# Batch 4's second FFN product by block products, and a new order of pieces, in an attention and maxout FFN kernel

## The chip, the cores and the metric

The kernel runs on one core of a Trainium2 chip. The metric is the device time of one execution in microseconds. The kernel before was timed in three runs: 163.65, 163.83 and 164.19 us, median 163.83. One further execution was profiled; it took 164.42 us.

A core has five engines with a queue of instructions each, in program order: TensorE (PE in the profile, with its weight loads as PEld) multiplies and writes to PSUM; VectorE (DVE), ScalarE (ACT) and GpSimd (POOL) do elementwise work; SyncE (SP) issues transfers. An instruction waits for semaphores before it starts, and whatever is queued behind it on its engine waits too.

## The reference

Inputs are q, k, v of shape (8 batches, 8 heads, 576 positions, 64) and phi of shape (8, 8, 576, 32), in float32. Per batch and head:

```python
a = softmax(phi, axis=2)              # over the 576 positions
k_m = a^T k ; v_m = a^T v             # (32, 64) each
attn = softmax(q k_m^T / 8, axis=-1)  # (576, 32)
o = attn v_m
```

The heads of a position are joined to a row x of 512, which gives 4608 rows, and then

```python
h = np.maximum(np.maximum(x @ w1, x @ w2), x @ w3)   # 512 -> 768
out = h @ w_out                                      # 768 -> 512
```

## The kernel before

The product of attn with v_m is never formed. Since x is attn times v_m, v_m is folded into the weights: per batch, small products of v_m with w1 - w3 and w2 - w3 give `wp`, and with w3 w_out give `wp3`. Then max(x w1, x w2, x w3) = x w3 + max(x (w1 - w3), x (w2 - w3), 0), so that FFN1 has two products instead of three (one evacuated with a Relu, the other with a max against it), and FFN2 adds attn times `wp3` to h times w_out.

The work is cut into pieces with names of a letter, a number and a batch. The same piece, such as `F8@2`, is a call of one helper. The order of all pieces is written out by hand as one list (line 758 on), and each engine's queue holds its instructions in the order of that list. A `!` behind a piece swaps the engine of its elementwise part. The letters that matter here:

- `L0` to `L3`: loads of phi, k, v, q (lines 86 to 115). They are issued by GpSimd; in two alternating buffers each, so a load waits until the batch two before has been read.
- `r0`, `r1`: packing of k and v (line 105), GpSimd, ScalarE when swapped. `E`: exponential of phi (232), ScalarE.
- `B`: the products a^T k and a^T v with their denominators (250). `N`: their normalisation on VectorE (263 to 292). `K`: transposes of the result on TensorE and an evacuation (294).
- `Q0`, `Q1`: transposes of q on VectorE (315). `S`: scores on TensorE (335) and two exponentials on ScalarE (344).
- `a`, `s`, `c`, `m`, `X`: the second softmax's transposition, sum, reciprocal (VectorE), product (`m`, line 411, GpSimd) and transposition back (VectorE, 419), in two halves 0 and 1.
- `D0` to `D3`: folds (442), evacuated mostly by ScalarE. `F0` to `F11`: FFN1 (468); an even number is evacuated with a Relu (ScalarE, VectorE when swapped), an odd one with the maximum (VectorE, 481).
- `T0` to `T4`: FFN2 of a tile of 128 positions (658, 667, 676), evacuated by either engine (EVAC at 167), and written to memory through SyncE. `T4` is the tile in the middle that two neighbouring batches share.

For the 512 positions of batches 5 and 6 outside `T4`, FFN2 is done as a two by two block product with seven products instead of eight. `U` combines the blocks of the weights (`combine_w`, 507; batch number 9 is for the shared w_out), `A0` to `A3` the blocks of h, 128 x 768, and `A4` to `A7` those of attn, 128 x 256 (`combine_a`, 552). All of them run through one helper at line 505, on GpSimd or VectorE. `P0` to `P6` (`products`, 565) are the seven products of 256 columns each (600), accumulated in place in three banks, with copies of intermediate states (612, 614) and sums into the output tile (641).

PSUM has eight banks. Which piece takes which bank is a string of digits (line 141); a piece whose bank hasn't been evacuated waits on TensorE.

Of the kernel before, what the change touches and what calls it, by code (L numbers as in the profile page):

```python
# [15 lines left out]
def kernel(  # L16
# [14 lines left out]
    B, H, S, D = q.shape  # L31
# [104 lines left out]
    for i in range(P // M):  # L136
# [4 lines left out]
    banks = iter(  # L141
        "".join(
            """
            00232204420145545045024602460260426042672643424260246024604260462342656204502406
            24062046204267240670462064260246024602064326247420640642064024620462042604605264
            620502645264034063460406064026042640246204203406767676
            """.split()
        )
    )
# [572 lines left out]
    def issue(b, n, swap):  # L722

        i = int(n[1:]) if len(n) > 1 else None
        {
            "I": lambda: [make_identity(nc, ident)]
            + [nc.gpsimd.memset(x[:, :, :, 2 * D : 2 * D + 1], 1.0) for x in kvrs],
            "Y": lambda: load_w(i) if i < 3 else load_wo(),
            "L": lambda: load_ph(b) if i == 0 else load_q(b) if i == 3 else load_kv(b, i - 1),
            "H": lambda: load_kv(b, i % 2, halves[i // 2]),  # L730
            "r": lambda: pack(b, i, swap),
            "E": lambda: [att_exp(b, h) for h in (halves if b == 0 else [slice(0, NP)])],
            "B": lambda: att_kv(b, i),
            "N": lambda: att_kv_norm(b, i),
            "K": lambda: att_kv_t(b, swap, i),
            "Q": lambda: att_q(b, i),
            "S": lambda: att_score(b),
            "a": lambda: att_t(b, i),
            "s": lambda: att_sum(b, i),
            "c": lambda: att_rec(b, i),  # L740
            "m": lambda: att_mul(b, i, swap),
            "X": lambda: (ones_mul if (b, i) in ONES else att_back)(b, i),
            "M": lambda: ones_sum(b, i),
            "R": lambda: ones_rec(b, i),
            "D": lambda: fold(b, i, swap),
            "F": lambda: ffn1(b, i, swap),
            "T": lambda: ffn2(b, i, swap),
            "U": lambda: combine_w(b, i, swap),
            "A": lambda: combine_a(b, i, not swap),
            "P": lambda: products(b, i, swap),  # L750
            "W": lambda: w3_t(i, swap),
            "O": lambda: w3_o(i, swap),
            "V": lambda: w_diff(i),
            "Z": lambda: warm_up(i),
        }[n[0]]()


    for w in """
        E@0 H2@0 H0@0 L3@0 Z25@0 B0@0 Y2@0 I@0 N0@0 Z2@0 K0@0! Q0@0 Q1@0 Z9@0 S@0 Z2@0
        M0@0 M1@0 R0@0 R1@0 W0@0 Y3@0 W1@0 W2@0 Z6@0 O1@0 H3@0 O3@0 O2@0 H1@0 X1@0 B1@0  # L760
        X0@0 N1@0 K1@0 O0@0 Y0@0 D1@0! D0@0! D3@0 F8@0 F10@0 F2@0 V0@0 F6@0 F0@0! Y1@0
        D2@0 D4@0 F4@0 L0@1 V1@0 F1@0 E@1 F3@0 L1@1 F5@0 F9@0 F7@0 L3@1 F11@0 B0@1 T3@0
        N0@1 K0@1! L2@1 Q1@1 L2@2 L1@2 Q0@1 L0@2 V2@0 T0@0! L3@2 S@1 T1@0 a0@1 s0@1 c0@1
        m0@1 B1@1 N1@1 a1@1 L1@3 K1@1 s1@1 D0@1 D1@1! D2@1 c1@1 m1@1 X0@1 L3@3 r1@2 X1@1
        T2@0! L2@3 F6@1 F10@1 F7@1 F2@1 F3@1 F4@1 F0@1 r0@2 E@2 F5@1 F1@1 F11@1 L0@3
        L0@4 F8@1 L2@4 F9@1 B@2 D3@1 N@2 Q1@2 T0@1! K@2 T2@1! r0@3 Q0@2 S@2 a0@2 a1@2
        s1@2 c1@2 m1@2 T4@1! D1@2! s0@2 D2@2 c0@2 m0@2 X1@2 D0@2 T3@1 Q0@3 L3@4 X0@2
        Q1@3 T1@1 F0@2 F4@2 F8@2 F6@2 F9@2 E@3 F7@2 F1@2 L1@4 r1@3 F10@2 F2@2 L2@5 B@3
        N@3 D3@2 F3@2 L1@5 F5@2 K@3! U0@9 F11@2 S@3 U1@9 E@4 T3@2 L0@5 T0@2! a1@3 D1@3!
        s1@3 D2@3 a0@3 r1@4 c1@3 L3@5 D0@3 T1@2 m1@3 s0@3 Q0@4 X1@3 c0@3 m0@3 X0@3 T2@2!  # L770
        F4@3! r0@4 F5@3 L2@6 F0@3 D3@3 B@4 F6@3 N@4 F1@3 F8@3 Q1@4 F2@3 F9@3 K@4! F10@3
        r1@5 F7@3 S@4 F11@3 L3@6 D3@4 E@5 r0@5 F3@3 a0@4 U3@9 L0@6 a1@4 T4@3! L1@6 L0@7
        s1@4 D0@4 D1@4! B@5 c1@4 N@5 T1@3 Q1@5 K@5 L1@7 Q0@5 s0@4 c0@4 m0@4 T3@3! S@5
        a0@5 T2@3! s0@5 a1@5 c0@5 X0@4 m1@4 X1@4 D2@4 D0@5 D1@5 m0@5 s1@5 X0@5 T0@3!
        F4@4 c1@5 F2@4 m1@5 r1@6 L2@7 F10@4 r0@6 F3@4 F5@4 F8@4 X1@5 F9@4 F0@4 F11@4
        F6@4 E@6 F10@5! F7@4 L3@7 F0@5 F2@5 A4@5! Q0@6 A5@5! F1@4 F1@5 A7@5! F8@5 F6@5
        F4@5! Q1@6 D3@5 B@6 N@6 r0@7 D2@5 T0@4! F7@5 F5@5 K@6 F3@5 U2@9 F9@5 U0@5! T1@4!
        F11@5 A0@5 A6@5 r1@7! E@7 S@6 T2@4! D1@6! U1@5! D2@6 a0@6 Q1@7 B@7 A1@5! U2@5
        U3@5 N@7 T3@4 s0@6 K@7! Q0@7 a1@6 P1@5 D3@6 s1@6 c1@6 S@7 c0@6 A2@5! m1@6 P2@5
        P4@5 a0@7 s0@7 D3@7 D2@7 m0@6 a1@7 c0@7 D1@7! P0@5! A3@5! U0@6 s1@7 P5@5 c1@7  # L780
        m1@7 X1@6 X0@6 T4@5! D0@6! D0@7 P6@5 U1@6 m0@7 F8@6 F9@6 F6@6 U3@6 U2@6 X0@7
        P3@5 F10@6 F2@6 X1@7 F11@6 F8@7 F0@6 F3@6 F7@6 F4@7 F1@6 F9@7 F4@6 A4@6 F5@6
        F2@7 F0@7 F5@7 A0@6! A6@6! A1@6! F6@7 F10@7! F3@7 A5@6! P1@6 A2@6! F1@7 P0@6
        F7@7 A3@6! F11@7 P2@6! P4@6 T0@7 T1@7 P5@6! A7@6 T4@7 P6@6! P3@6! T2@7! T3@7
    """.split():
        n, b = w.rstrip("!").split("@")
        issue(int(b), n, w.endswith("!"))
# [30 lines left out]
```

## Time and profile before

| | us |
|---|---|
| median of three runs | 163.83 |
| lowest and highest | 163.65, 164.19 |
| profiled execution | 164.42 |
| its span, first to last instruction | 162.4 |
| TensorE busy | 152.6 |
| VectorE busy | 104.5 |
| ScalarE busy | 97.8 |
| GpSimd busy | 92.2 |

The granted clock of TensorE was 0.998 on average. In the profile, L468 is a line of the kernel, PE, DVE, ACT and POOL are the engines, and a row of the timeline has the start and the length in us, then engine, line, operation, output and inputs, and in brackets the idle time before it and what ended it. In the chain of waits a row has start, length and the work that the end hung on at that time. The ends of matmuls are modelled, so their lengths overlap in the timeline; starts are exact.

### The profile page before, as it was taken

What the parts mean: (1) busy time and instruction counts of PE and PEld (TensorE: products, weight loads), DVE (VectorE), ACT (ScalarE), POOL (GpSimd) and SP (SyncE); (2) the same over time, 40 slices, a digit from 0 to 9 for tenths busy, and PEclk for the clock granted to TensorE, in tenths of its full rate; (3) what the DMA queues carried; (4) which work ended last, traced back from release to release, by engine and by line L of the source; (5) the groups of instructions that cost most, each with busy time, mean ns of one, the idle gap of its engine ahead of it and who ended that gap; (6) DMA issues with size and microseconds to landing.
All of it is one profiled execution on the core that took longest, in us unless ns stands there. A gap on an engine that the chain in (4) does not pass through costs nothing.

```text
span 162.4 us, 4946 instructions
## 1 busy us (share of the span) xinstructions
PE 152.6 (94%) x2128; PEld 90.5 (56%) x2128; DVE 104.5 (64%) x201; ACT 97.8 (60%) x144; POOL 92.2 (57%) x92
## 2 busy tenths in 40 slices
PE   7958798999798999999999999999999999999991
PEld 2433544673366535753584536776456577785570
DVE  2013703898837847577487797986999967874340
ACT  4204535934497468977689849688779786631110
POOL 7931115100598359899877964999094880395000
PEclk9999999999999999999999999999999999999999
DMA  5999999999999999999999999999221044000365
GB/s 153 152 205 208 206 211 214 276 208 210 250 323 232 212 244 378 261 237 205 261 318 230 212 312 306 286 183 174 84 96 65 4 164 160 4 0 0 129 253 199
DMA packets 21909, 31.76 MB, mean 196 GB/s; under 512 B 1152, under 2 KB 16512, under 8 KB 21888
## 3 DMA queue, kind: packets, MB, share of 16 engines
q0 software_dynamic: 16080, 21.43, 69.1%
q1 hardware_dynamic: 5664, 9.90, 17.3%
q8 instruction: 16, 0.26, 0.6%
q10 hardware_dynamic: 144, 0.13, 0.2%
q14 instruction: 5, 0.04, 0.1%
HBM read 39.32 MB, written 9.44 MB: 300 GB/s over the span
## 4 chain that ended last, share of the span: by engine, by line
PE 62%; DMA 27%; DVE 4%; POOL 3%; ACT 1%; issue 1%; POOLq 0%
PE psum L468 22%; PE psum L658 17%; DMA ph<-in_phi_dram 15%; DMA w_sb<-in_moe_w_dram 12%; PE psum L600 8%; PE psum L667 5%; PE psum L442 4%; PE psum L250 2%; POOL kvo L98 2%; PE psum L676 1%; PE psum L335 1%; DVE twb L505 1%; PE psum L699 1%; ACT e L232 1%; PE psum L300 1%
## 5 line engine op out<-in xcount | busy, mean ns | idle before, releaser
L468 PE MATMUL psum<-attn,wp 128*128 128x288 bf16 x384 | 50.2, 286 | 0.2
L468 PEld LDWEIGHTS <-wp 128*128 128x128 bf16 x384 | 36.9, 98 | 12.0 <-issue 1.5
L481 DVE TENSOR_TENSOR hT<-psum,h 128x576 bf16<-128x576 f32 x48 | 34.5, 752 | 12.7 <-PE psum L468 8.3
L658 PE MATMUL psum<-wo_sb,hT 128*128 128x512 bf16 x162 | 39.6, 380 | 0.0
L173 ACT ACTIVATE h<-psum 128x576 bf16<-128x576 f32 x43 | 26.1, 657 | 7.2 <-PE psum L468 7.1
L175 ACT CAST wp<-psum 128x1024 bf16<-128x1024 f32 (+1 forms) x30 | 28.4, 996 | 2.6 <-PE psum L442 2.6
L175 ACT COPY ot<-psum 128x512 f32<-128x512 f32 x23 | 13.6, 591 | 23.2 <-PE psum L667 18.2
L411 POOL TENSOR_TENSOR t<-t,sm 128x576 bf16<-128x576 bf16 x14 | 16.1, 1154 | 19.2 <-DVE sm L406 19.2
L108 POOL COPY kvr<-kvo 128x2304 bf16<-128x2304 bf16 x11 | 23.2, 2111 | 5.5 <-DMA kvo<-in_k_dram 4.4
L658 PEld LDWEIGHTS <-hT 128*128 128x128 bf16 x162 | 14.6, 98 | 17.8 <-issue 3.2
L667 PE MATMUL psum<-wp,attn 128*128 128x512 bf16 x46 | 13.7, 379 | 0.0
L344 ACT ACTIVATE e<-psum 128x576 bf16<-128x576 f32 x16 | 9.6, 653 | 6.1 <-PE psum L335 6.1
L162 PE MATMUL psum<-warm 128*128 128x512 bf16 x44 | 12.1, 428 | 1.2 <-DVE warm L131 1.2
L315 DVE STREAM_TRANSPOSE qT<-qq 128x576 f32<-128x576 f32 x16 | 12.0, 760 | 1.1 <-DMA qq<-in_q_dram 1.0
L232 ACT ACTIVATE e<-ph 128x1152 bf16<-128x1152 f32 (+1 forms) x9 | 9.5, 1061 | 2.9 <-DMA ph<-in_phi_dram 2.7
L98 POOL DMA_DIRECT2D kvo<-in_v_dram x9 | 6.8, 753 | 7.4 <-PE psum L250 4.1
L397 DVE TENSOR_REDUCE sm<-t 128x18 f32<-128x576 bf16 x14 | 10.4, 740 | 0.2
L113 POOL DMA_DIRECT2D qq<-in_q_dram x8 | 6.1, 759 | 6.3 <-DMA w_sb<-in_moe_w_dram 6.0
L250 PEld LDWEIGHTS <-e 64*32 64x32 bf16 x720 | 7.1, 90 | 4.5 <-issue 2.8
L389 DVE STREAM_TRANSPOSE t<-e 128x288 f32<-128x288 f32 x14 | 6.5, 468 | 4.0 <-ACT e L344 4.0
L98 POOL DMA_DIRECT2D kvo<-in_k_dram x9 | 6.9, 769 | 2.9 <-DMA qq<-in_q_dram 2.1
L419 DVE STREAM_TRANSPOSE attn<-t 128x288 f32<-128x288 f32 x14 | 6.2, 456 | 3.5 <-POOL t L411 3.5
(94 smaller groups left out, 181.0 us busy)
## 6 DMA issues: line engine op xcount, KB each, us to landing
out_dram<-ot SPq DMA_DIRECT2D x27, 256.0 KB, 6.0
qq<-in_q_dram POOLq DMA_DIRECT2D x8, 576.0 KB, 14.0
ph<-in_phi_dram POOLq DMA_DIRECT2D x7, 576.0 KB, 16.0
kvo<-in_k_dram POOLq DMA_DIRECT2D x7, 576.0 KB, 15.9
kvo<-in_v_dram POOLq DMA_DIRECT2D x7, 576.0 KB, 16.7
w_sb<-in_moe_w_dram POOLq DMA_DIRECT2D x3, 768.0 KB, 19.4
out_dram<-oj SPq DMA_DIRECT2D x4, 512.0 KB, 2.8
wo_sb<-in_moe_w_out_dram POOLq DMA_DIRECT2D x1, 768.0 KB, 15.0
```

What stands on the lines that cost most here:

```text
L98: nc.gpsimd.dma_start(out=kv[:, i, h].rearrange("p j c d -> p j (c d)"), in_=by_pair((k, v)[i], b)[:, h],)
L108: nc.gpsimd.tensor_copy(out=out_, in_=in_)
L162: nc.tensor.matmul(po[:, 0:BANK], lhsT=warm[:, 0:P], rhs=warm, start=True, stop=True)
L173: nc.scalar.activation(out=out_, in_=in_, func=AF.Relu)
L175: nc.scalar.copy(out=out_, in_=in_)
L315: nc.vector.transpose(out=s["qT"][:, j].rearrange("p j c r e -> p (j c r e)").bitcast(FP32), in_=loaded[b]["q"][:, j].rearrange("p j c d - ...
L411: (nc.vector if swap else nc.gpsimd).tensor_tensor(out=t, in0=t, in1=s["sm", g].unsqueeze(2).to_broadcast([P, S // HP, R, 2]), op=ALU.mult,)
L468: nc.tensor.matmul(acc[:, h, 0:SH], lhsT=wps[b][:, g, w * DF + ft * P : w * DF + (ft + 1) * P], rhs=attn[:, g, c0 : c0 + SH], start=(g == ...
L481: nc.vector.tensor_tensor(out=hT[:, ft, (b % 2) * S : (b % 2 + 1) * S].rearrange("p (h n) -> p h n", h=2), in0=a, in1=s["h1", ft], op=ALU.max,
L600: nc.tensor.matmul(po[:, q * CH : (q + 1) * CH], lhsT=lhs(k, q), rhs=rhs(k), start=(i < 3 and k == 0 and q == 0), stop=(k == KT and q == 1 ...
L658: nc.tensor.matmul(po, lhsT=hT[:, fc, c0 : c0 + P], rhs=wo_sb[:, fc, :], start=(n == 0), stop=False,)
L667: nc.tensor.matmul(po, lhsT=attn[:, g, c0 : c0 + P], rhs=wp3s[b][:, g, :], start=False, stop=(g == NG - 1),)
```

## The change

Only two texts of the kernel change: the list of pieces behind the first 91, and the string of banks that goes with it. FFN2 of batch 4 is no longer done by `T0@4` to `T3@4`, but by `U0@4` to `U3@4`, `A0@4` to `A7@4` and `P0@4` to `P6@4`, as batches 5 and 6 are. All other pieces stay, in another order and in part with another engine. The list grows from 402 to 417 pieces. Of the combinations, VectorE keeps one (`A6@6`) of the six it had, and the others are on GpSimd. `r0@5` goes to ScalarE beside `r1@7`. The loads behind `L1@3` come in the order v, phi, q of 3; v, k, phi, q of 4; k, phi, v of 5; k of 6, q of 5; v, phi, q of 6; phi, v, k, q of 7. Before, it was q, v, phi of 3; phi, v, q, k of 4; v, k, phi, q of 5; v, q, phi, k of 6; phi, k, v, q of 7.

```diff
-            00232204420145545045024602460260426042672643424260246024604260462342656204502406
...
+            00232204420145545045024602460260426042672643424260240642046204620160247402672062
...
-        m0@1 B1@1 N1@1 a1@1 L1@3 K1@1 s1@1 D0@1 D1@1! D2@1 c1@1 m1@1 X0@1 L3@3 r1@2 X1@1
-        T2@0! L2@3 F6@1 F10@1 F7@1 F2@1 F3@1 F4@1 F0@1 r0@2 E@2 F5@1 F1@1 F11@1 L0@3
-        L0@4 F8@1 L2@4 F9@1 B@2 D3@1 N@2 Q1@2 T0@1! K@2 T2@1! r0@3 Q0@2 S@2 a0@2 a1@2
-        s1@2 c1@2 m1@2 T4@1! D1@2! s0@2 D2@2 c0@2 m0@2 X1@2 D0@2 T3@1 Q0@3 L3@4 X0@2
...
+        m0@1 B1@1 N1@1 a1@1 L1@3 K1@1 s1@1 D0@1 D1@1! D2@1 c1@1 m1@1 L2@3 X0@1 X1@1 T2@0
+        L0@3 F0@1! F6@1 F10@1! F7@1 F8@1 F4@1 F2@1 F5@1 r1@2 r0@2 F11@1 E@2 L3@3 F9@1
+        F1@1 F3@1 B@2 U0@9 U1@9 N@2 D3@1 Q1@2 Q0@2 T1@1! K@2! r0@3 T0@1! D0@2! S@2 T4@1!
+        L2@4 a0@2 s0@2 L1@4 c0@2 a1@2 s1@2 c1@2 D2@2 D3@2 m0@2 L0@4 X0@2 m1@2 X1@2 D1@2!
+        r1@3 E@3 T3@1! T2@1! F8@2 U3@9 F10@2 F9@2 F0@2 F6@2 Q1@3 B@3 Q0@3 N@3 F2@2 F4@2
+        L3@4 L1@5 F3@2 F1@2 K@3! L0@5 F7@2 F11@2 L2@5 S@3 F5@2 a1@3 D3@3 a0@3 r1@4 s1@3
+        c1@3 r0@4 s0@3 m1@3 D0@3 E@4 T1@2 T0@2! D1@3! D2@3 c0@3 X1@3 B@4 N@4 m0@3 T2@2!
+        X0@3 Q0@4 K@4! L1@6 Q1@4 F10@3! F0@3 F2@3 F1@3 S@4 L3@5 L2@6 L0@6 U2@9 F3@3 a1@4
+        F8@3 s1@4 D3@4 U0@4 D1@4! D0@4 c1@4 a0@4 s0@4 T3@2 m1@4 c0@4 F11@3 m0@4 F9@3
+        F4@3 F6@3 X0@4 X1@4 F5@3 F7@3 F4@4! F0@4! T2@3 r0@5! E@5 F1@4 r1@5 D2@4 B@5 F2@4
...
+        A2@4! X1@5 T4@3! S@6 E@7 L3@7 A1@4! D0@6! P0@4! A3@4! a1@6 a0@6 s1@6 F6@5 A6@4!
+        F4@5 F2@5 s0@6 P1@4! F8@5 F0@5 r0@7 r1@7! P2@4 F9@5 F5@5 P4@4 c0@6 U2@5 F3@5
+        F10@5 B@7 c1@6 m0@6 U0@5 D3@6 N@7 F1@5 P3@4! K@7! F7@5 U2@4 A4@5! F11@5 P5@4
...
+        P4@6 F11@7 F5@7 P0@6 T1@7! A6@6 P3@6 T4@7 U3@6 P5@6 T2@7 P6@6 T0@7 T3@7
```

More of the change, by code (lines that the diff above doesn't have):

```diff
@@ L143 @@
             """
-            00232204420145545045024602460260426042672643424260246024604260462342656204502406
-            24062046204267240670462064260246024602064326247420640642064024620462042604605264
-            620502645264034063460406064026042640246204203406767676
+            00232204420145545045024602460260426042672643424260240642046204620160247402672062
+            40246204602406236042340620462046204602640240624026402340626024674274026402740240
+            40240420240620460247024020202406240260247204247237237
             """.split()
@@ L763 @@
         N0@1 K0@1! L2@1 Q1@1 L2@2 L1@2 Q0@1 L0@2 V2@0 T0@0! L3@2 S@1 T1@0 a0@1 s0@1 c0@1
-        m0@1 B1@1 N1@1 a1@1 L1@3 K1@1 s1@1 D0@1 D1@1! D2@1 c1@1 m1@1 X0@1 L3@3 r1@2 X1@1
-        T2@0! L2@3 F6@1 F10@1 F7@1 F2@1 F3@1 F4@1 F0@1 r0@2 E@2 F5@1 F1@1 F11@1 L0@3
-        L0@4 F8@1 L2@4 F9@1 B@2 D3@1 N@2 Q1@2 T0@1! K@2 T2@1! r0@3 Q0@2 S@2 a0@2 a1@2
-        s1@2 c1@2 m1@2 T4@1! D1@2! s0@2 D2@2 c0@2 m0@2 X1@2 D0@2 T3@1 Q0@3 L3@4 X0@2
-        Q1@3 T1@1 F0@2 F4@2 F8@2 F6@2 F9@2 E@3 F7@2 F1@2 L1@4 r1@3 F10@2 F2@2 L2@5 B@3
@@ L769 @@
[L769 to L784, printed above, removed]
+        m0@1 B1@1 N1@1 a1@1 L1@3 K1@1 s1@1 D0@1 D1@1! D2@1 c1@1 m1@1 L2@3 X0@1 X1@1 T2@0
+        L0@3 F0@1! F6@1 F10@1! F7@1 F8@1 F4@1 F2@1 F5@1 r1@2 r0@2 F11@1 E@2 L3@3 F9@1
@@ new lines @@
+        F8@3 s1@4 D3@4 U0@4 D1@4! D0@4 c1@4 a0@4 s0@4 T3@2 m1@4 c0@4 F11@3 m0@4 F9@3
+        F4@3 F6@3 X0@4 X1@4 F5@3 F7@3 F4@4! F0@4! T2@3 r0@5! E@5 F1@4 r1@5 D2@4 B@5 F2@4
+        N@5 F10@4 F8@4 Q1@5 F5@4 A4@4! F11@4 L3@6 F3@4 A5@4! F6@4 K@5! Q0@5 U1@4 A7@4!
+        T1@3! S@5 a0@5 E@6 F9@4 L0@7 s0@5 T0@3! c0@5 r0@6 F7@4 U3@4 r1@6 L2@7 m0@5 B@6
+        D2@5 D1@5! N@6 T3@3 a1@5 s1@5 L1@7 A0@4! K@6 c1@5 Q1@6 Q0@6 X0@5 D3@5 m1@5 D0@5
+        A2@4! X1@5 T4@3! S@6 E@7 L3@7 A1@4! D0@6! P0@4! A3@4! a1@6 a0@6 s1@6 F6@5 A6@4!
@@ new lines @@
+        F4@5 F2@5 s0@6 P1@4! F8@5 F0@5 r0@7 r1@7! P2@4 F9@5 F5@5 P4@4 c0@6 U2@5 F3@5
+        F10@5 B@7 c1@6 m0@6 U0@5 D3@6 N@7 F1@5 P3@4! K@7! F7@5 U2@4 A4@5! F11@5 P5@4
+        D1@7 A5@5! Q1@7 D2@7 U1@5 Q0@7 D3@7 T4@5! D1@6! m1@6 D2@6! X0@6 D0@7 A7@5! P6@4
+        X1@6 A6@5! P1@5 S@7 F4@6! P2@5! A0@5! F0@6 a1@7 a0@7 F1@6 s0@7 A1@5! c0@7 s1@7
+        P0@5 F8@6 c1@7 P4@5 A2@5! U3@5 A3@5! F10@6 m0@7 F6@6 P5@5! m1@7 F2@6 F9@6 A4@6!
+        X1@7 P3@5! U0@6 X0@7 F3@6 P6@5 F5@6 F2@7 U2@6 F7@6 F8@7 A5@6! A7@6! U1@6 F11@6
@@ L785 @@
+        F6@7 F0@7! P1@6! A0@6! F9@7 F7@7 A1@6! A2@6! A3@6! F10@7! P2@6 F3@7 F4@7 F1@7
+        P4@6 F11@7 F5@7 P0@6 T1@7! A6@6 P3@6 T4@7 U3@6 P5@6 T2@7 P6@6 T0@7 T3@7
     """.split():
```

## The prediction

> **What bounds the kernel now.** I read the page's first part, then the busy time by stretches, then the chain that ended last.
>
> ```profile
> span 162.4 us, 4946 instructions
> PE 152.6 (94%) x2128; PEld 90.5 (56%) x2128; DVE 104.5 (64%) x201; ACT 97.8 (60%) x144; POOL 92.2 (57%) x92
> ```
>
> ```profile
> 70.00:90.00 20.00, 19.93 (x297) 10.89 (x302) 14.72 (x29) 15.90 (x24) 16.91 (x13) 1.00 1.18 247
> 90.00:110.00 20.00, 20.00 (x344) 12.55 (x326) 17.18 (x34) 14.69 (x22) 16.14 (x17) 1.00 1.14 260
> 110.00:130.00 20.00, 19.95 (x310) 11.50 (x308) 18.11 (x39) 15.43 (x21) 12.99 (x11) 1.00 0.31 82
> ```
>
> Columns: stretch, length, then busy time of TensorE, weight loads, VectorE, ScalarE and GpSimd, granted clock, DMA share. TensorE has practically no idle time and the full clock, so a microsecond taken from its work, or added as a wait of it, is a microsecond of the time. The DMA engines are full (share above 1) until 110, and VectorE is the next engine to fill up: 18.1 of 20 us in the last stretch. The chain of waits gives the pieces of the TensorE stream:
>
> ```profile
> 51.36 1.17 ACT e L232
> 52.58 0.80 PE psum L250 x69
> ...
> 70.75 0.49 ACT kvt L175
> ...
> 96.92 0.77 PE psum L442 x24
> 97.70 1.40 PE psum L658 x6
> ...
> 121.03 0.53 DVE kvn L285 x2
> ...
> 133.71 8.82 PE psum L468 x72
> 142.53 0.87 PE psum L600 x8
> ...
> 147.49 1.29 PE psum L658 x6
> 148.79 0.43 PE psum L667 x2
> 149.22 1.29 PE psum L658 x6
> ```
>
> The reader sees prices (start, length). One block product (L600, eight matmuls of 256 columns): 0.87 us. One token tile of FFN2 (L658 and L667, eight of 512 columns): 149.22 - 147.49 = 1.73. Eighteen FFN1 pieces: 8.82, so 0.49 each. Behind folds, which use small tiles of the array, the first six matmuls of a token tile take 1.40, not 1.29. The links of other engines are TensorE's waits: at 51.36 the exponential of batch 2's phi, before B@2; at 70.75 ScalarE's copy of kvt, before S@3; at 121.03 VectorE's kvn, before K@7.
>
> **The change, part by part.** *TensorE's work.* T0@4 to T3@4 go: 4 x 1.73 = 6.92. P0@4 to P6@4 come: 7 x 0.87 = 6.09. Net -0.83 us, all of it on the path. A rule speaks against this. The Trainium skill (TensorE: Matmul & The Clock Gate, Back-to-back issue gap) gives a sustained spacing of about 81 ns for 128 columns and 131 ns for 512, thus an estimate near 98 ns for 256; by it 56 narrow matmuls (5.5 us) cost 1.3 us more than 32 wide ones (4.2), and the time would come out near 165.4. The trace does not agree: 0.87/8 = 109 ns and 1.73/8 = 216 ns, in proportion to the columns, for these very pieces; that case gets no chance.
>
> *Order on TensorE.* The old list comes back from small tiles to full size 25 times behind D2@1, the new one 24 times: -0.11 (1.40 less 1.29). The waits at 70.75 and 121.03 have causes that the new list removes: between K@3 and S@3 stood one FFN1 piece and now stand two; and kvn was late for K@7 because VectorE had been held for 1.5 us just before (below). By the start of the next piece they cost 0.2 each. I take -0.4 and keep 0 as the other end. The wait of B@2 stays: in front of it stand T2@0 and the same twelve FFN1 pieces, and its phi is issued in the unchanged part.
>
> *Work of the other engines.*
>
> ```profile
> L505 POOL TENSOR_TENSOR w_sb<-w_sb,hT 128x768 bf16<-128x768 bf16 x2 | 3.3, 1640 | 4.5 <-DVE w_sb L505 4.5
> L505 POOL TENSOR_TENSOR twb<-wp 128x256 bf16<-128x256 bf16 x3 | 2.1, 685 | 0.0
> L641 DVE TENSOR_TENSOR oj<-psum,snap 128x512 f32<-128x512 f32 x4 | 2.8, 692 | 0.3 <-PE psum L600 0.2
> L179 DVE CAST wp<-psum 128x1024 bf16<-128x1024 f32 x3 | 3.6, 1211 | 2.2 <-PE psum L442 2.2
> ```
>
> GpSimd: five more large combinations (1.64) and twelve more small ones (0.68), one packing copy (2.1) fewer: +14 us to 106, spread over 60 to 146. Counted along its queue, A0@4 is done 2 us ahead of P0@4, U2@4 (behind r0@7, U2@5, m0@6, U0@5) 1 us ahead of P5@4, U3@6 4 us ahead of P6@6. I cost this at nothing; if r0@7's load comes a microsecond late, that cover is gone and P5@4 waits. VectorE: three block sums, two snapshots and nine evacuations that ScalarE did (14 x 0.7), two casts (1.21); less two small copies, one block copy and five of its six own combinations (4.5 together): +7.7. ScalarE loses about 5.
>
> ```profile
> 117.81 1.64 POOL L505 TENSOR_TENSOR w_sb<-w_sb,hT 128x768 bf16<-128x768 bf16 x1 [4.52 <-DVE w_sb L505]
> 117.84 1.75 DVE L505 TENSOR_TENSOR twb<-wp,twb 128x256 bf16<-128x256 bf16 x1
> ```
>
> VectorE's small combination (a third of the large one's columns) started 0.03 us behind GpSimd's large one and ended 0.14 us behind it: it was held. The Trainium skill (SBUF — State Buffer, Who interferes with whom) has it that of two such operations the later is blocked for the whole of the first; the trace agrees. The new list leaves one on VectorE, A6@6, beside U3@6 (0.68): at most as long again, while its reader P5@6 comes some 3 us later. What is gained is VectorE's time, no TensorE time of its own: 0.
>
> *New waits.* Batch 2's normalising products stand on GpSimd behind more DMA issues:
>
> ```profile
> 57.64 2.11 POOL L108 COPY kvr<-kvo 128x2304 bf16<-128x2304 bf16 x1 [3.31 <-DMA kvo<-in_k_dram]
> 61.09 2.27 POOL L411 TENSOR_TENSOR t<-t,sm 128x576 bf16<-128x576 bf16 x2 [1.34 <-DVE sm L406]
> 63.32 0.79 POOL L113 DMA_DIRECT2D qq<-in_q_dram  x1
> ...
> 82.72 2.11 POOL L108 COPY kvr<-kvo 128x2304 bf16<-128x2304 bf16 x1 [0.87 <-DMA kvo<-in_v_dram]
> ```
>
> r0@3 still starts with the landing at 57.64 and ends at 59.75; L2@4 and L1@4 (0.75 each) bring 61.25, m0@2 62.4, L0@4 63.1, m1@2 64.25, X1@2 (0.45) 64.7. TensorE, running on behind B@2 at 52.58 by the prices above, reaches the second half of F8@2, which reads it, at 64.4: +0.3. ScalarE is the second place:
>
> ```profile
> 58.21 1.20 ACT L344 ACTIVATE e<-psum 128x576 bf16<-128x576 f32 x2
> ...
> 60.26 2.85 ACT L175 CAST wp<-psum 128x1024 bf16<-128x1024 f32 x3
> ...
> 64.62 2.28 ACT L173 ACTIVATE h<-psum 128x576 bf16<-128x576 f32 x4
> ```
>
> Around S@4 (TensorE at 81.4 to 81.8) its queue holds F0 and F2 of batch 3 (0.57 each), two exponentials (1.20), F8 and three casts (2.85) in nearly one run from 80.5 to 86.6; F4@3, reached at 86.3, wants the bank that the last cast empties: +0.3. VectorE, busy 35.3 of 40 us between 90 and 130 and with its share of the +7.7, is left little slack: +0.2. The three together lie between 0 (the list runs without a gap, as the old one nearly does) and 1.4 (every operation as long as if alone; in these rows successive ones overlap by some 0.05). I take 0.8.
>
> *Loads.* Phi of batch 4 now goes behind q of 3, v of 4 and k of 4.
>
> ```profile
> L94 POOL DMA_DIRECT2D ph<-in_phi_dram x1: 753/753/753, 52.8 to 52.8; - x1
> DMA to landing us min/median/max: 16.0/16.0/16.0
> ```
>
> It landed at 68.8. E@4 now needs it for B@4, which TensorE reaches at 76.5, and on ScalarE T1@2, T0@2, D1@3 and D2@3 queue behind E@4. Loads land in the order of issue: from 57.64 to 82.72 eight came, 3.1 us each. I take 1.9 for a phi (they are written unconverted) and 3.5 for another, which makes 24.8 of the 25.1. Behind 57.64 the new order has v, phi, q, v, k, phi: 4 x 3.5 + 2 x 1.9 = 17.8, landing at 75.4, and E@4 (1.17) ends at 76.6. I cost it at nothing, but the slack is nil.
>
> *Sum.* On the profiled execution (164.42, of which 162.4 span): -0.83 - 0.11 - 0.4 + 0.8 = -0.54, so 163.88. That execution stands 0.59 above the median of the runs, 163.83; so 163.3. The tail behind the last matmul is the same pair of half tiles.
>
> **The rivals.** *Clean run:* none of the new waits occurs: -1.34, 162.5. For it: the old list has few waits behind B@2. Against: the 64.7 above is a sum without a free term. *Phi of batch 4 lands late (the other side):* with 4.3 us for v and k of 4 and 3.5 for the rest, phi lands at 77.0, E@4 ends at 78.2 and B@4 starts 1.5 late, ScalarE's tiles and casts with it; part of the waits counted above falls away in that time, so +1.3: 164.6. Against: the share of DMA is full in both orders, the mean holds for eight loads. It turns the sign from 0.55 us late on (landing at 75.9). *VectorE becomes the bound* between 90 and 130: that takes 4.7 of its 7.7 added us in those 40, each further one is TensorE's; 5.7 there would make +1.0, less the 0.2 counted: 164.1. For it: 18.1 of 20 already. Against: of the nine evacuations that it takes over, only those of T2@3, T1@3 and F4@6 lie there.
>
> **How the numbers follow.** Forecast 0.45, clean run 0.15, late phi 0.2, VectorE 0.2. The likeliest alone lies between 162.8 and 163.8. For 8 in 10 the range reaches to the clean run below and just past the late phi above: 162.4 to 164.8. A measurement of this kernel can tell 0.3%, 0.49 us, from no change. Faster than 163.34: the clean run and 0.30 of the forecast, 0.45. Within: the rest of the forecast and most of VectorE's case, 0.29. Slower than 164.32: late phi and what VectorE's case has above, 0.26.
>
> **What would show it.** After: 24 matmuls of 512 columns fewer at L658 and 56 more at L600, at the same 1.29 and 0.87; no VectorE combination before 140; the exponential at 51.4 still before B@2; a wait under 0.5 us at the first FFN1 piece of batch 2, another near 86; E@4 starting at 75 to 75.8. I am wrong if E@4 starts behind 76, if TensorE waits on VectorE between 95 and 125, or if TensorE has idle time at places that I did not name.

## The result and the profile after

The changed kernel took 162.90 us in the median of 13 runs (162.41 to 163.45), the kernel before 163.76 in 13 runs (163.01 to 164.72). The ratio is 0.9943, with a 95% interval of 0.9926 to 0.9961: faster by 0.86 us, where 0.5 was forecast. Its profiled execution took 162.73 us, of which 160.9 is span. (Executions more than 1.5% above the fastest of the same kernel do not count in the ratios.)

The first part of its page:

```profile
span 160.9 us, 5023 instructions
PE 152.0 (94%) x2152; PEld 93.0 (58%) x2152; DVE 110.9 (69%) x209; ACT 93.5 (58%) x135; POOL 106.0 (66%) x108
```

The busy time by stretches of the changed kernel, with the columns of the prediction (TensorE, weight loads, VectorE, ScalarE, GpSimd, granted clock, DMA share, GB/s):

```profile
70.00:90.00 20.00, 19.81 (x294) 11.39 (x295) 17.22 (x34) 17.92 (x24) 16.35 (x15) 1.00 1.17 258
90.00:110.00 20.00, 20.00 (x365) 11.90 (x363) 16.90 (x35) 15.22 (x22) 17.99 (x17) 1.00 1.12 253
110.00:130.00 20.00, 20.00 (x303) 14.49 (x301) 17.46 (x32) 14.92 (x21) 18.51 (x19) 1.00 0.40 107
```

TensorE is still the engine that sets the end: no idle time at all from 90 to 130, a little before. GpSimd has become nearly as full (18.5 of 20) without holding anybody up, and VectorE has more work in all (110.9 against 104.5) but less of it in the last stretch (17.46 against 18.11).

The groups and the chain of waits of the changed kernel give the prices again. The first row is the kernel before's, for the count:

```profile
L658 PE MATMUL psum<-wo_sb,hT 128*128 128x512 bf16 x162 | 39.6, 380 | 0.0
```

```profile
L658 PE MATMUL psum<-wo_sb,hT 128*128 128x512 bf16 x138 | 33.7, 380 | 0.0
L505 POOL TENSOR_TENSOR w_sb<-w_sb,hT 128x768 bf16<-128x768 bf16 x3 | 4.9, 1649 | 0.2
L505 DVE TENSOR_TENSOR sa<-attn 128x256 bf16<-128x256 bf16 x1 | 0.3, 282 | 0.0
```

```profile
111.36 0.87 PE psum L600 x8
112.24 0.98 PE psum L468 x8
113.22 0.87 PE psum L600 x8
...
145.88 1.29 PE psum L658 x6
147.61 0.87 PE psum L600 x8
```

There are 24 matmuls fewer at L658 (138 for 162), a product costs 0.87 us and two FFN1 pieces 0.98, as before; a token tile is 147.61 - 145.88 = 1.73. VectorE keeps one combination, of 0.28 us.

Two profiles can be compared piece by piece: the start of each piece is read from the trace of each kernel, and where one kernel has lost time shows as a step in the difference. In the two profiles shown so far the start of the last piece, `T3@7`, moved by -1.61 us (157.08 to 155.47). That is more than the medians say. Of it, 0.24 was there before the kernels' lists differ in anything, and 0.58 is the wait of B@2, of which more below. What remains, 0.79, lies behind B@2.

### The profile page after: what moved, and what is told of

Same layout as the page of the kernel before. It is cut to its first block, busy times and chain, and to the rows that moved or that the text cites. A ratio compares the mean times of both kernels' runs of the same rounds, so it can differ in the third digit from the quotient of the medians.

```text
span 160.9 us, 5023 instructions
## 1 busy us (share of the span) xinstructions
PE 152.0 (94%) x2152; PEld 93.0 (58%) x2152; DVE 110.9 (69%) x209; ACT 93.5 (58%) x135; POOL 106.0 (66%) x108
## 4 chain that ended last, share of the span: by engine, by line
PE 82%; DMA 9%; DVE 2%; POOL 2%; issue 1%; ACT 1%; DVEq 0%; POOLq 0%
PE psum L468 29%; PE psum L658 19%; PE psum L600 12%; DMA wo_sb<-in_moe_w_out_dram 9%; PE psum L667 5%; PE psum L442 5%; PE psum L250 4%; PE psum L195 3%; PE psum L335 2%; PE psum L676 1%; DVE hT L481 1%; POOL kvo L98 1%; PE psum L699 1%; PE psum L300 1%; DVE h L177 0%
## 5 line engine op out<-in xcount | busy, mean ns | idle before, releaser
L468 PE MATMUL psum<-attn,wp 128*128 128x288 bf16 x384 | 52.2, 286 | 0.4 <-DVE hT L481 0.2
L658 PE MATMUL psum<-wo_sb,hT 128*128 128x512 bf16 x138 | 33.7, 380 | 0.0
L175 ACT CAST wp<-psum 128x1024 bf16<-128x1024 f32 (+1 forms) x28 | 26.3, 993 | 7.2 <-PE psum L442 7.2
L173 ACT ACTIVATE h<-psum 128x576 bf16<-128x576 f32 x39 | 23.8, 656 | 10.9 <-PE psum L468 10.9
L108 POOL COPY kvr<-kvo 128x2304 bf16<-128x2304 bf16 x10 | 21.1, 2117 | 4.1 <-DMA kvo<-in_k_dram 2.1
L658 PEld LDWEIGHTS <-hT 128*128 128x128 bf16 x138 | 12.4, 98 | 15.3 <-issue 3.4
L162 PE MATMUL psum<-warm 128*128 128x512 bf16 x44 | 12.8, 445 | 1.2 <-DVE warm L131 1.2
L175 ACT COPY ot<-psum 128x512 f32<-128x512 f32 x14 | 8.1, 589 | 8.0 <-PE psum L667 6.7
L667 PE MATMUL psum<-wp,attn 128*128 128x512 bf16 x38 | 11.3, 379 | 0.0
L179 DVE COPY ot<-psum 128x512 f32<-128x512 f32 x9 | 6.2, 684 | 6.6 <-PE psum L667 4.4
L162 PEld LDWEIGHTS <-warm 128*128 128x128 bf16 x44 | 4.5, 111 | 7.3 <-issue 3.5
```

The costliest lines, as they stand in the source:

```text
L108: nc.gpsimd.tensor_copy(out=out_, in_=in_)
L162: nc.tensor.matmul(po[:, 0:BANK], lhsT=warm[:, 0:P], rhs=warm, start=True, stop=True)
L173: nc.scalar.activation(out=out_, in_=in_, func=AF.Relu)
L175: nc.scalar.copy(out=out_, in_=in_)
L468: nc.tensor.matmul(acc[:, h, 0:SH], lhsT=wps[b][:, g, w * DF + ft * P : w * DF + (ft + 1) * P], rhs=attn[:, g, c0 : c0 + SH], start=(g == ...
L658: nc.tensor.matmul(po, lhsT=hT[:, fc, c0 : c0 + P], rhs=wo_sb[:, fc, :], start=(n == 0), stop=False,)
```

## The experiments

All were timed beside the kernel before on the same chip; the ratio given is to that. "Level with the changed kernel" means that the same pieces start at the same time in the two traces, apart from a constant that is already there before B@2.

**The same two kernels again.** No edit; the changed kernel (with timing) and the kernel before (one profiled execution).

> The changed kernel once more, for a second profile. If batch 2's phi lands about 1.3 us earlier because of the change, it does so again and B@2 has no wait; if that was the draw of one execution, B@2 shows a wait of up to 0.7 us here or the kernel before shows none in its next profile. Time 0.9 us below the kernel before in both cases.

> The kernel before once more, for a second profile. If the late phi of batch 2 belongs to the kernel before, B@2 waits here too, 0.5 us or more; if it was one execution's draw, B@2 has no wait and the time is some 0.6 us below the first profile's.

The changed kernel took 162.94 (ratio 0.9948, 0.9924 to 0.9972), so the result stands. The profiled execution of the kernel before took 163.33, with a span of 161.4. ScalarE's and the weight loads' timeline around B@2, in the first profile of the kernel before:

```profile
51.36 1.16 ACT L232 ACTIVATE e<-ph 128x1152 bf16<-128x1152 f32 x1 [1.01 <-DMA ph<-in_phi_dram]
...
52.57 0.66 PEld L250 LDWEIGHTS <-e 64*32 64x32 bf16 x72 [0.82 <-ACT e L232]
```

in the second profile of the same kernel:

```profile
49.68 1.17 ACT L232 ACTIVATE e<-ph 128x1152 bf16<-128x1152 f32 x1
...
51.43 0.67 PEld L250 LDWEIGHTS <-e 64*32 64x32 bf16 x72 [0.24 <-issue]
```

and in the changed kernel:

```profile
50.03 1.18 ACT L232 ACTIVATE e<-ph 128x1152 bf16<-128x1152 f32 x1
...
51.75 0.66 PEld L250 LDWEIGHTS <-e 64*32 64x32 bf16 x72 [0.24 <-issue]
```

In the first profile phi of batch 2 landed 3.07 us behind the load ahead of it (51.34 after 48.26), and the exponential stood 1.01 us waiting for it. In the second it landed 1.54 us behind (49.59 after 48.05), the exponential followed ScalarE's earlier work without a wait, and B@2 started on time. So the list of pieces alone doesn't bring the wait of B@2: it belonged to that one execution. With it removed, the comparison is between the second profile of before and the profile of after: B@2 to `T3@7` takes 104.63 us in the one and 103.72 in the other, a gain of 0.91, and the medians give 0.86 to 0.93. The other pairings of the two profiles of each kernel give 0.73, 0.79 and 0.85, so this gain is known to some 0.1 us.

**T2@0 on ScalarE.** The changed kernel has VectorE evacuate this early tile, ahead of B@2; this undoes it.

```diff
-X0@1 X1@1 T2@0 L0@3 F0@1! F6@1 F10@1!
+X0@1 X1@1 T2@0! L0@3 F0@1! F6@1 F10@1!
```

> The changed kernel with T2@0 evacuated by ScalarE, as before the change (one token of the list). If the earlier landing of batch 2's phi (49.7 instead of 51.1) comes from T2@0's store or its evacuation, phi lands near 51 again and B@2 waits 0.5 to 0.7 us: as much slower than the changed kernel. If it comes from another part of the new order, nothing changes.

Measured 163.38 (0.9984, 0.9961 to 1.0007), 0.4 to 0.5 above the changed kernel. TensorE's timeline in it:

```profile
47.66 5.06 PE L468 MATMUL psum<-attn,wp 128*128 128x288 bf16 x40 [0.21 <-ACT ot L175]
```

`F10@1` now waits for the bank of T2@0, and everything behind starts 0.37 us later up to the end. B@2 has no wait here either (its weight loads show 0.24 of issue as above, at 52.65): phi of batch 2 landed at 50.03, 1.55 behind the load ahead of it, so who evacuates T2@0 has nothing to do with that landing.

**The new order without the products.** The changed kernel with `U`, `A` and `P` of batch 4 taken out and T0@4 to T3@4 put at the places of four products, in three spacings. The first has them at P0, P1, P2 and P3:

```diff
-... D0@6! P0@4! A3@4! a1@6 ... s0@6 P1@4! F8@5 F0@5 r0@7 r1@7! P2@4 F9@5 F5@5 P4@4 c0@6 ...
-... F1@5 P3@4! K@7! F7@5 U2@4 A4@5! F11@5 P5@4 D1@7 ... A7@5! P6@4 X1@6 ...
+... D0@6! T0@4 a1@6 ... s0@6 T1@4! F8@5 F0@5 r0@7 r1@7! T2@4! F9@5 F5@5 c0@6 ...
+... F1@5 T3@4 K@7! F7@5 A4@5! F11@5 D1@7 ... A7@5! X1@6 ...
```

> The new order, but FFN2 of batch 4 by four token tiles again (where P0, P1, P2 and P3 of batch 4 stood; the combinations of batch 4 are left out). My account (the gain is TensorE's work): TensorE gets 4 x 1.73 - 7 x 0.87 = 0.83 us back, so 0.8 us slower than the changed kernel, within 0.3 us of the kernel before. Rival (the new order carries the gain by itself, and the block products' saving is lost in waits): as fast as the changed kernel, 0.9 us faster than before.

Measured 165.64 (1.0125, 1.0089 to 1.0160), 2.7 above the changed kernel, while the four tiles are only 0.83 us more of TensorE work. It is level with the changed kernel up to D0@6 (106.6). From its timeline:

```profile
112.12 0.69 DVE L179 COPY ot<-psum 128x512 f32<-128x512 f32 x1 [0.47 <-PE psum L667]
115.38 1.42 DVE L481 TENSOR_TENSOR hT<-psum,h 128x576 bf16<-128x576 f32 x2 [2.58 <-PE psum L468]
...
116.19 1.32 PE L468 MATMUL psum<-attn,wp 128*128 128x288 bf16 x8 [0.43 <-DVE hT L481]
...
122.30 0.63 PE L442 MATMUL psum<-w_sb,kvt 64*32 64x512 bf16 x16 [0.36 <-DVE hT L481]
```

VectorE is idle for 2.58 us while TensorE works through a whole tile and the FFN1 pieces that ScalarE evacuates. Then two pieces with a maximum come in close succession, VectorE (0.75 us for each) can't follow TensorE (0.49), and TensorE waits for a bank. The second version spreads the tiles, at the places of P0, P2, P3 and P6:

```diff
-P0@4! ... P1@4! ... P2@4 ... P4@4 ... P3@4! ... P5@4 ... P6@4
+T0@4 ... ... T1@4 ... ... T2@4 ... ... T3@4
```

> As e1, but the four token tiles of batch 4 stand where P0, P2, P3 and P6 of batch 4 stood, so that TensorE's stream never runs ahead of the changed kernel's and VectorE has fewer operations. If e1's surplus over 0.83 us came from TensorE reaching pieces before VectorE had emptied their banks, it is gone here: 0.83 us (0.6 to 1.1) above the changed kernel, level with the kernel before. If plain token tiles cost more than 1.73 us in this order, or the order needs the block products for another reason, it stays near 2.5 us above the changed kernel.

Measured 165.11 (1.0082, 1.0054 to 1.0111), 2.2 above. TensorE's waits and one stretch of it:

```profile
114.56 1.31 PE L468 MATMUL psum<-attn,wp 128*128 128x288 bf16 x8 [0.43 <-DVE hT L481]
...
120.66 0.63 PE L442 MATMUL psum<-w_sb,kvt 64*32 64x512 bf16 x16 [0.36 <-DVE hT L481]
```

```profile
110.00:130.00 20.00, 18.95 (x265) 11.11 (x266) 13.95 (x26) 13.93 (x20) 15.89 (x15) 1.00 0.39 109
```

The same two waits are left, before F3@5 and before D1@7: where P4@4 and P5@4 stood. By the starts of the pieces they cost 0.58 and 0.42, and the pieces behind them, F10@5 and D3@7, wait another 0.18 and 0.23; with the 0.83 of work that makes the 2.2. The third version puts tiles at just those places, P1, P4, P3 and P5:

```diff
-P0@4! ... P1@4! ... P2@4 ... P4@4 ... P3@4! ... P5@4 ... P6@4
+... T0@4 ... ... T1@4 ... T2@4 ... T3@4 ...
```

> The new order with plain tiles of batch 4 again, now at the places of its products 1, 4, 3 and 5 (the earlier spread stood at 0, 2, 3 and 6). Theory: taking the products back costs their 0.83 us of TensorE work; the other 1.4 us of the spread version were waits on VectorE in two stretches where FFN1 pieces with a maximum then stand close together, F9, F5, F3 and F7, F11 of batch 5, because products 4 and 5 no longer stand between them. With a tile at those two places the waits before F3@5 and before D2@7 go, and the time is 0.8 to 1.3 us above the changed kernel: 163.7 to 164.2. Rival: seven places of TensorE work are needed to keep VectorE in step, and four cannot do it wherever they stand: 1.8 us or more above, 164.7 to 165.3.

The theory fell; the loss is the rival's 1.8 us or more, and beyond the range that it gave: 165.99 (1.0144, 1.0106 to 1.0181), 3.1 above. TensorE's timeline and the same stretch:

```profile
107.58 1.68 PE L468 MATMUL psum<-attn,wp 128*128 128x288 bf16 x12 [0.48 <-ACT e L344]
...
112.22 1.20 PE L468 MATMUL psum<-attn,wp 128*128 128x288 bf16 x8 [0.25 <-ACT h L173]
...
120.39 1.14 PE L468 MATMUL psum<-attn,wp 128*128 128x288 bf16 x8 [0.61 <-DVE ot L179]
```

```profile
110.00:130.00 20.00, 18.83 (x260) 10.49 (x259) 12.77 (x22) 13.13 (x18) 15.90 (x15) 1.00 0.38 107
```

The waits before F3@5 and D1@7 are gone, and others have come: each time at an FFN1 piece that wants the bank of a piece shortly before it. F6@5 wants one of S@6's, which an exponential empties, and P0 no longer stands between; F9@5 wants that of F8@5's Relu, and P2 no longer stands between; F7@5 wants that of T2@4 itself, which is a choice of this version. By the starts these cost 0.5, 0.4 and 0.8 us, and S@7 and F4@6, which stand where P6 was, wait another 0.4; with the smaller ones 2.4 us, which is what the 3.2 us by the starts leave beside the 0.83 of work. VectorE is less busy here than in the changed kernel (12.8 of 20 against 17.5), and TensorE waits more. So it isn't the amount of work on VectorE or ScalarE that holds TensorE up, but how soon a bank is wanted again after the piece that fills it. The changed kernel's list has a piece of 0.87 us at seven places where something stands between the two; four tiles of 1.73 at four of these places leave others bare. The FFN1 pieces kept their banks in all three versions. Whether a list of its own with plain tiles, or other banks in this one, would lose only the 0.83 was not tried; what the three runs show is that this list, with these banks, can't do without its products.

**The products without the new order.** The kernel before with `U`, `A` and `P` of batch 4 put in, and batch 5's combinations moved behind batch 4's products.

```diff
+... m1@4 U0@4 U1@4 U2@4 U3@4 ... A4@4! A5@4! ... A6@4! A7@4! ... r0@7 A0@4! A1@4! ... A3@4! A2@4! ...
-... T0@4! ... T1@4! ... T2@4! ... T3@4 ...
+... P1@4 ... P2@4 ... P0@4 P4@4 ... P3@4 P5@4 P6@4 A0@5 A4@5! A5@5! A7@5! A6@5 A1@5! ...
```

> The old order with FFN2 of batch 4 by block products put in where its token tiles stood (their combinations on GpSimd, those of batch 5 moved behind them). My account: TensorE's work falls by 0.83 us, but GpSimd has no room between 109 and 125 (8 combinations of 1.64 us and two more of 0.67 on top of r0 of 7 and U2 of the shared weights), so P0, P4 and the products of batch 5 wait: 1 to 4 us slower than before. Rival (the products bring their gain in any order): 0.5 to 0.9 us faster than before.

Measured 166.99 (1.0188, 1.0139 to 1.0237), 3.2 slower than the kernel before. Its timeline:

```profile
110.29 2.10 POOL L108 COPY kvr<-kvo 128x2304 bf16<-128x2304 bf16 x1
...
119.05 0.83 PE L600 MATMUL psum<-wo_sb,w_sb 128*128 128x256 bf16 x6 [0.84 <-POOL w_sb L505]
...
120.64 0.83 PE L600 MATMUL psum<-w3T,hT 128*128 128x256 bf16 x6 [0.55 <-POOL hT L505]
...
122.47 0.82 PE L600 MATMUL psum<-w3T,hT 128*128 128x256 bf16 x6 [0.78 <-DVE oj L641]
```

Up to there it is 0.5 ahead of the second profile of before, and at those three products it loses 2.7 (0.99, 0.72 and 0.95 by the starts of the pieces): GpSimd packs k of batch 7 from 110.29 and forms the combinations only then, and the third product waits for VectorE's sum. Together with the runs before it this says that neither half of the change, as built here, is worth anything alone.

**The four large combinations of batch 4 on VectorE.**

```diff
-A0@4! ... A2@4! ... A1@4! ... A3@4!
+A0@4 ... A2@4 ... A1@4 ... A3@4
```

> The changed kernel with the four large combinations of h of batch 4 on VectorE instead of GpSimd. My account: VectorE gets 4 x 0.56 more between 102 and 112, and each one that starts inside an operation of GpSimd is held up to 1.6 us, so lengths of 1 to 2 us; VectorE is full there, so TensorE waits for it, 0.5 to 2 us above the changed kernel. Rival (no holding, or slack enough): lengths of 0.56 and no change of the time.

Measured 163.68 (0.9995, 0.9968 to 1.0022), 0.74 above the changed kernel; the profiles put it 0.51 behind. Two of its groups and two stretches:

```profile
L505 DVE TENSOR_TENSOR hT<-hT 128x768 bf16<-128x768 bf16 x1 | 0.8, 800 | 0.0
L505 DVE TENSOR_TENSOR w_sb<-hT,w_sb 128x768 bf16<-128x768 bf16 x1 | 0.5, 541 | 0.0
```

```profile
90.00:110.00 20.00, 19.75 (x359) 11.67 (x360) 18.01 (x36) 15.04 (x22) 13.36 (x14) 1.00 1.14 252
110.00:130.00 20.00, 19.83 (x300) 14.23 (x299) 17.96 (x33) 14.72 (x21) 16.48 (x16) 1.00 0.39 109
```

The four take 0.54 to 0.80 us each on VectorE, where GpSimd needs 1.64; this is 2.5 us of VectorE's time, and by the starts TensorE loses 0.16 us at T4@3, 0.07 at F2@5, 0.12 at F3@5 and 0.17 at F10@5. A hold as long as the 1.75 us that the prediction quotes did not happen to any of them: GpSimd had no large combination running beside them. The two longest, 0.80 and 0.62 (the others took 0.54 and 0.55), are the two that overlap its small combination at 106.82, and that one took 0.88 us instead of 0.67. So what the two-operand work costs on VectorE here is mostly its length, at places without slack, and being held adds at most some 0.3 us.

**Phi of batch 4 one load later.**

```diff
-D3@2 m0@2 L0@4 X0@2 ... F4@2 L3@4 L1@5
+D3@2 m0@2 X0@2 ... F4@2 L3@4 L0@4 L1@5
```

> The changed kernel with the issue of batch 4's phi one load later, behind q of 4. My account (loads land in the order of issue, B@4 has 0.3 us of slack): phi lands at about 76.9 instead of 74.3, E@4 ends at 78.1, B@4 starts 2.3 us late, time 2.0 to 2.4 us above the changed kernel, so 1 to 1.5 us slower than before. Rival (the queues and banks absorb it): within 0.5 us of the changed kernel.

Measured 166.82 in the median of the four executions that the ratio is taken from (1.0177, 1.0125 to 1.0230; over all six 167.19), 3.9 above the changed kernel. Phi landed at 76.87 instead of 74.20. TensorE's timeline, and its stretches from there:

```profile
78.17 0.81 PE L250 MATMUL psum<-kvr,e 64*32 64x129 bf16 x72 [2.04 <-ACT e L232]
```

```profile
76.00:78.00 2.00, 0.12 (x8) 0.00 (x0) 0.23 (x1) 1.05 (x1) 2.00 (x3) 1.00 1.20 233
78.00:79.00 1.00, 0.83 (x73) 0.76 (x74) 0.00 (x0) 1.00 (x4) 1.00 (x2) 1.00 1.13 320
79.00:80.00 1.00, 0.85 (x3) 0.39 (x4) 0.94 (x5) 1.00 (x3) 1.00 (x3) 0.62 1.11 330
80.00:82.00 2.00, 2.00 (x6) 0.64 (x5) 1.74 (x4) 0.90 (x1) 1.49 (x1) 0.50 1.22 228
82.00:83.00 1.00, 1.00 (x9) 0.83 (x8) 0.00 (x0) 0.75 (x2) 0.00 (x0) 0.67 1.09 265
83.00:85.00 2.00, 2.00 (x47) 1.30 (x45) 1.04 (x2) 1.41 (x3) 0.00 (x0) 1.00 1.12 277
```

By the starts of the pieces B@4 is 2.2 us late, and by S@4 it is 3.9: the other 1.7 are no wait. A microsecond after the wait the granted clock fell to 0.50 and stayed there for 3.4 us, in which half of the work, 1.7 us, is lost, and the token tile T2@2 took 3.10 us instead of 1.73. One of the six executions had a mean clock of 0.997 instead of 0.988 or 0.989 and took 165.14, about what the wait alone would give.

**Phi of batch 4 two loads earlier.**

```diff
-S@2 T4@1! L2@4 a0@2 s0@2 L1@4 c0@2 ... m0@2 L0@4 X0@2
+S@2 T4@1! L0@4 L2@4 a0@2 s0@2 L1@4 c0@2 ... m0@2 X0@2
```

> The changed kernel with the load of phi of batch 4 issued ahead of v and k of 4 instead of behind them. If landing late is a risk of phi alone, phi lands 6 to 7 us earlier (67 instead of 74) and the time stays, 162.8 to 163.0. If loads land in the order of issue, k of 4 takes phi's place in the line: it lands at 73.9 instead of 72.4, its packing on GpSimd ends at 76.3 instead of 74.8, and TensorE waits 0.6 us at B@4, which the end keeps: 163.4 to 163.7.

Measured 163.86 (1.0005, 0.9982 to 1.0029). Its profile is 0.51 us behind the changed kernel from K@4 on: by the starts 0.26 at B@4 and 0.27 at the first piece behind K@4, a little of which is made up later. GpSimd's timeline in it

```profile
74.97 2.11 POOL L108 COPY kvr<-kvo 128x2304 bf16<-128x2304 bf16 x1 [0.72 <-DMA kvo<-in_k_dram]
```

and in the changed kernel

```profile
72.67 2.11 POOL L108 COPY kvr<-kvo 128x2304 bf16<-128x2304 bf16 x1 [0.99 <-DMA kvo<-in_k_dram]
```

Phi landed at 67.89 and k of 4 took its place in the line: its packing starts 2.3 us later on the page, 1.2 of it against the start of the kernel, whose first part was 1.1 us longer in this execution. Phi, v and k of a batch are one queue with one deadline, and the order that the change has is the better of the two. (The median is 0.9 above the changed kernel's; beyond 0.5 it isn't shown by the profile.)

**The new wait at S@3, in two attempts.** The changed kernel has a wait that the kernel before hadn't (below): F5@2, the piece behind S@3, waits for VectorE behind five maxima in a row. (The expectations call a wait by the piece ahead of it: their S@3 is the wait of F5@2, their F5@2 that of D3@3.) This moves F3@2 ahead of F4@2, so that VectorE can start 0.29 us earlier; in the first version each keeps its bank, in the second the two change banks.

```diff
-N@3 F2@2 F4@2 L3@4 L1@5 F3@2 F1@2 K@3! L0@5 F7@2 F11@2 L2@5 S@3 F5@2
+N@3 F2@2 F3@2 F4@2 L3@4 L1@5 F1@2 K@3! L0@5 F7@2 F11@2 L2@5 S@3 F5@2
```

> The changed kernel with F3@2 one place earlier, ahead of F4@2 (their banks with them). Theory: the wait of S@3 is VectorE's backlog of five maxima in a row, which began 0.29 us late because F3 came half a microsecond after VectorE was free; now it starts at once, the wait at S@3 shrinks from 0.27 us to about 0 and that at F5@2 from 0.11 to 0, and the time is 0.2 to 0.35 lower, 162.5 to 162.7. Rival: phi of batch 4, which lands 0.3 us before it is needed, takes it back: a wait of 0.1 to 0.3 us at B@4 and no change, 162.8 to 163.0.

> The same swap of F3@2 and F4@2, but now the two also change banks, so that F7@2 takes the bank that VectorE empties with F3 (by 68.9 us) instead of the one that ScalarE empties with F4 (69.1). Theory: in the swap before, the 0.30 us at F7@2 was the bank of F4's late Relu alone; now F7 waits 0.1 at most, VectorE runs its five maxima from 68.1 without a gap, the waits at S@3 (0.27) and F5@2 (0.11) fall to 0.1 together, and the time is 0.1 to 0.3 below the changed kernel, 162.6 to 162.8. Rival: B@4 then waits on phi of batch 4, which lands at 74.0 whatever stands here, and the time is the changed kernel's, 162.85 to 163.0.

Neither gained: 163.23 (0.9973, 0.9947 to 0.9998) and 163.28 (0.9973, 0.9947 to 1.0000), both a little above the changed kernel; the profiles put them 0.31 and 0.07 behind it. In the first, ScalarE's timeline shows why:

```profile
68.46 0.65 ACT L173 ACTIVATE h<-psum 128x576 bf16<-128x576 f32 x1 [0.39 <-PE psum L468]
```

That is F4's Relu, half a microsecond later than before, and F7@2 waits 0.30 for its bank. In the second F7@2 doesn't wait, VectorE runs from 68.19 without a gap, and F5@2 comes at once. Then TensorE's timeline has

```profile
71.35 0.41 PE L442 MATMUL psum<-w3o,kvt 64*32 64x512 bf16 x8 [0.20 <-ACT e L344]
```

D3@3 waits for the bank of the scores, until ScalarE's exponential is through. By the starts D3@3 waits 0.27 there, as long as F5@2 did before. So two waits end at nearly the same time, and taking away one shows the other. B@4, which the rival named, shows no wait in either.

## Why the prediction was right, and where it was not

The forecast was 163.3 with a range of 162.4 to 164.8; the time came out 0.4 lower, between the forecast and the "clean run" of 162.5.

*TensorE's work, -0.83.* Right: the products are 0.87, the tiles 1.73, and the rule that narrow matmuls cost more than their share of the columns (the Trainium skill, TensorE: Matmul & The Clock Gate, Back-to-back issue gap) would have put the time near 165.4; the trace of after does not agree with it: its products take 109 ns a matmul again.

*Order, -0.11.* Wrong. The counts of 25 and 24 come out if the transposes `K` are taken for small tiles. They aren't; their weights are 128 x 128:

```profile
68.55 0.28 PEld L300 LDWEIGHTS <-kvn 128*128 128x128 bf16 x3
```

Without them both lists come back from folds, scores and the products of `B` to full size 19 times, and the term is nothing.

*Order, -0.4.* Right in the main. The waits on kvt and kvn are gone, and they were 0.23 and 0.21 by the starts of the pieces in the second profile of before. Of the 0.23, though, 0.09 is no wait: an FFN1 piece ahead of small tiles takes 0.58 instead of 0.49 at the other such places of both lists too. So 0.35 was removed.

*"The wait of B@2 stays."* Wrong. It is absent from the profile after, and from the second profile of the kernel before with an unchanged list. The argument from the list was sound, but the wait wasn't in the list. It did no harm to the number, because the sum was brought from its own execution (164.42) down to the median (163.83), 0.59 lower, and that wait was 0.58. This is luck: the second profile of before, which has no such wait, took 163.33, another 0.5 less, so executions differ by as much for other reasons.

*Other engines, nothing.* Right: GpSimd's busy time is 106.0 as counted, VectorE's 110.9 (112.2 counted) and ScalarE's 93.5 (92.8), and TensorE has no idle time in the stretch of the products. The experiment with the large combinations on VectorE shows the other side: there was no slack for them there. The cover of r0@7 held.

*New waits, +0.8.* This term was mis-sized, and none of its three places was right. From the changed kernel's timeline:

```profile
63.43 1.76 PE L468 MATMUL psum<-attn,wp 128*128 128x288 bf16 x13
...
68.46 3.59 DVE L481 TENSOR_TENSOR hT<-psum,h 128x576 bf16<-128x576 f32 x5 [0.29 <-PE psum L468]
...
70.60 0.65 PE L468 MATMUL psum<-attn,wp 128*128 128x288 bf16 x4 [0.19 <-DVE hT L481]
...
74.28 1.17 ACT L232 ACTIVATE e<-ph 128x1152 bf16<-128x1152 f32 x1 [0.69 <-DMA ph<-in_phi_dram]
```

F8@2 starts at 63.43 without a wait: the 64.7 for what it reads was counted from loads of an execution in which, as is now known, phi of batch 2 had held the line up by 1.5 us. At F4@3 there are less than 0.1, and VectorE between 90 and 130 holds nothing up. In their place F5@2 waits 0.27, a place that the prediction passed over with "now stand two": it looked at what stands ahead of S@3 for kvt and not at the five maxima that then follow each other on VectorE. With small ones of 0.07 to 0.08 at T1@1, F8@3 and F6@3 that makes some 0.5.

*The sum.* The old list had small waits too, 0.16 to 0.26 in its two profiles, so that 0.5 to 0.6 us of waits went and about 0.5 came. What is left is TensorE's work, -0.83, where the profiles have -0.73 to -0.91 and the medians -0.86. The prediction had the mechanism, and its order and waits made a loss of 0.29 together where the traces show about none; that is most of the 0.4 between forecast and result.

*Loads.* Right: 17.8 us were counted from the landing of the load that r0@3 waits for to that of phi of 4; 56.23 to 74.20 is 17.97. E@4 started at 74.28, a microsecond ahead of the forecast, for the reason just given (the loads stood 1.4 us earlier), and B@4 had about 0.3 to spare.

*The rivals.* VectorE as the bound did not occur. Phi of 4 landing late did not either, but the run with it one load later shows that the prediction had its price too low: 2.2 us of waiting cost 3.9, since the clock falls behind it. At the 1.5 us late that the rival assumed this wasn't tried.

## What to carry to other kernels

A wait that is seen in one profile may belong to that execution and not to the program: profile the same kernel a second time before a step of the argument is built on the wait or on landings behind it. Where TensorE has no idle time, as here, the order of pieces is a spacing of bank users, so an alternative for one kind of piece can't be priced by its own length in a list made for the other; both halves of this change lose alone. A removed wait is worth only the distance to the next one at the same place, here 0.0 of 0.27 us. Whether a piece uses small tiles of the array is read from the shapes in the trace, not from what the piece is for.

## What the runs showed of the hardware that was not expected

A single wait of TensorE of 2.0 us, in a stream that had run at full clock, brought the granted clock from 1.00 to 0.50 about a microsecond after work had begun again, for 3.4 us, and cost 1.7 us beside the wait. This is seen in one profile; that it happened in five of the six executions is read from their mean clock of 0.988 or 0.989. (Of the 86 executions of the kernel before that ran beside the experiments, five have a mean clock of 0.985 to 0.990 too. They were not profiled, and where their clock fell is not known.) Waits of up to 1.27 us never did that in these traces; the longest stands at the start of the kernel before, at a granted clock of 1.00:

```profile
9.81 0.80 PE L250 MATMUL psum<-kvo,e 64*32 64x128 bf16 x72 [1.27 <-DMA kvo<-in_k_dram]
```

The Trainium skill (TensorE: Matmul & The Clock Gate, Part 1: The HAM clock gate) has a gate with only a full and a half clock, which drops after an idle window of about 3.4 us that runs freely and rises after a busy one of the same length. The half clock and its 3.4 us agree; that 2.0 us of idleness were enough does not follow from the rule as it stands. The ends of the kernels point the same way: in the fourteen profiles the half clock comes 2.3 to 5.4 us after the last matmul.

The start varies: in the profiles of ten executions whose lists are the same up to B@2, B@2 starts at 51.59 to 52.85 us with no wait ahead of it, which is more than the effect under study. In the latest of them TensorE had waited 1.10 us for a load of `w_sb` at 31.5, which the changed kernel's profile hasn't. What made phi of batch 2 land 1.5 us late in one execution is not shown by any run.
